# The second MLP in two sweeps over its column groups: partial sums through DRAM, weight conversions moved into the first sweep

## Chip, cores and metric

The kernel runs on one core of a Trainium2 chip. The metric is the device time of one execution in microseconds (us). The engines are TensorE (PE: matmuls; PEld: its weight loads), VectorE (DVE), ScalarE (ACT), GpSimd (POOL) and SyncE (SP), whose queue issues nearly all DMAs of this kernel.

## Reference

Three parts follow each other: an attention over the 256 channels of 6016 tokens, an MLP with squared ReLU (width 2048), and an MLP with an RMS norm and a SiLU gate (width 1536). Cut to what matters here:

```python
def _moe_ref(x, w_in, w_out):                      # first MLP
    h = np.maximum(x @ w_in, 0.0)
    return (h * h @ w_out)

def _moe2_ref(x, w_gate, w_val, w_out, rms_g):     # second MLP
    rms = np.sqrt(np.mean(x * x, axis=-1, keepdims=True) + 1e-06)
    xn = x / rms * rms_g
    g = xn @ w_gate
    silu = g * (1.0 / (1.0 + np.exp(-g)))
    val = xn @ w_val
    return (silu * val @ w_out)
```

## The kernel before, in words

The tokens are worked through in six pairs of blocks: five pairs of 2 x 512 tokens and a last one of 2 x 448 (numbered 0 to 5). The channels lie on the partitions, the tokens along the free dimension. After the attention (to about 57 us) comes the first MLP (to about 568 us), then the second (to about 1100 us).

Every fp32 value is kept as two fp32r numbers, a high and a low part, and a product of two such values takes three matmuls. In the second MLP the pair of token blocks and the halves of gate and value form a 2 x 2 problem that is done in seven products in place of eight; for it each pair has seven operands (x itself and sums of it), kept in DRAM (`xd`) with high and low part. A **visit** is the work of one pair, in 12 **groups** of 128 columns of the width. A group (`group` in `mlp2`, from L1501) has 21 matmuls of 512 columns for the seven products (L1528) and 12 "down" matmuls by the output weights (`mm3`, L110 to L112), which add to four sums in PSUM over all groups of the visit. Between them ScalarE copies banks (L1581, L1594, L1595, L1605), applies SiLU (L1601, L1638) and casts high parts (L1627), and VectorE joins products (L1606, L1615, L1620, L1641) and forms low parts (L1631). The last four down products of a visit are issued in the first group of the next; each is copied by ScalarE (L1516) into a tile `ys`, and from there transposed by VectorE (L1672) and stored (L1679).

The weights of the second MLP come as raw words and have to be converted by the kernel. Gate and value weights are cut in six chunks of 256 columns (0 to 5, one for two groups), the output weights in six parts of rows (0 to 5). A conversion is a row of steps: the load of 512 KB (L134), two decoding steps on GpSimd and ScalarE (L142, L145: step "a"), three on VectorE (L149, L153, L157: "b" and "c"), for a value chunk the sums of its halves (L303 to L308: "d" and "e"), then high parts on ScalarE (L216, L175: "h") and low parts on VectorE (L222, L182: "l"). Chunk 0 is kept in SBUF. `STREAMED = 3` and `EARLY = 3` say that chunks 1 to 3 and parts 0 to 3 are converted during the first MLP and put into DRAM (`gvd`, `w2d`), from where they are loaded at the start of the second MLP. Chunks 4 and 5 and parts 4 and 5 (late parts 0 and 1) are converted beside the groups of pair 0's visit. Their order is written out by hand: the string `SIDE2` (L1992) is a list of tokens, "4ga" being step a of the gate half of chunk 4, "0c+1load" step c of late part 0 followed by the load of late part 1, "." an empty place. `group` takes tokens from this list at five fixed places (`aside`, `asides`), each on the engine that the token names.

Of the seven operands the next visit needs, the first three (products 0, 3 and 1) are fetched behind group 4 (L2035), for odd pairs in one tile (`xs`, L1174), for even ones in single tiles (L1164); the other four follow in the last group, each as soon as the product that read its tile is done. The last pair's RMS norm and operands are made late: its first-MLP result waits in DRAM (`yd`), and in the visit of pair `XLATE = 2` the steps of `pair_norm` (L983, with L1009 and L1024) and `pair_steps` (L1086, with L1101 to L1113) are appended to the list behind group 3; in that visit the fetch of the next operands comes behind group 10. The store of its last operand stands ahead of that fetch in SP's queue:

```python
if f == (10 if p == XLATE else 4) and p + 1 < NP:
    for i in ORDER[:3]:
        fetch(p + 1, i, nxt)
```

Of the kernel before, what the change touches and what calls it, by code (L numbers as in the profile page):

```python
# [20 lines left out]
P = 128  # L21
# [7 lines left out]
def attn_moe_kernel(ctx: ExitStack, tc, q, k, v, tau, w_in, w_out, w_gate, w_val, w2, rms_g, out):  # L29
# [158 lines left out]
    HELD = 1  # L188
    EARLY = 3
    ROWS = EARLY + 1  # L190
    STREAMED = 3
    gv, gv_dram = {}, {}
# [73 lines left out]
    class LateRows(Call):  # L266
# [6 lines left out]
        def take(self):  # L273
            if "raw" not in late_tiles:
                late_tiles.update(raw=own["raw"][2].rearrange("p a n -> p (a n)").bitcast(I32), g=own["dg"][2])
            self.raw, self.g = late_tiles["raw"], late_tiles["g"]

# [1222 lines left out]

    def mlp2(p, ops, after_product, after_group, side):  # L1501
        n = blocks[2 * p][1]
        o = {}
        left, lasts = [], {}

        def down(f, t, d, ph, pl):
            def g():
                assert f // 2 < ROWS or ("w2", f // 2) in formed, f
                if f == 0:
                    o[t, d] = acc(d)[:, :n]  # L1510
                wh, wl = (tiles[w][:, f, d].rearrange("p i e -> p (i e)") for w in ("w2_h", "w2_l"))
                mm3(o[t, d], wh, wl, ph, pl, f == 0, f == NF2 - 1)
                if f == NF2 - 1 and p < NP - 1:
                    if d == 0:
                        o[t] = xp.tile([P, KC, NB], F32, tag="ys", name="ys", bufs=2)
                    nc.scalar.copy(out=o[t][:, d, :n], in_=o[t, d])  # L1516

            return g

        def group(f):  # L1520
# [75 lines left out]
            late("p2")  # L1596
            if f:
                aside("dve")
# [10 lines left out]
            if side and getattr(side[0], "takes_bank", False):  # L1609
                side.pop(0)(b0)()  # L1610
                rooted.append(f)
            elif f:
# [3 lines left out]
            if f:  # L1616
                asides()
# [66 lines left out]

        return group, left, last_down, finish

# [177 lines left out]
    def as_raw(t):  # L1864
        return t.rearrange("p a n -> p (a n)").bitcast(I32)
# [59 lines left out]
    for p in range(FIRST, NP):  # L1925
# [15 lines left out]
        def after_product(g, i):  # L1941
            if g == NF1 // 2 - 1:
                if not last and i in ORDER[3:]:
                    fetch_v(p + 1, i, nxt)
                if last and i == 0:
                    fetch(0, 4, ops0)
                if p == FIRST and i == ORDER[-1]:
                    wide_steps.pop(0)()
                    wide_steps.pop(0)()
                if p == NP - 2 and i == 0:  # L1950
                    last_chunk["vload"]()

        def after_group(g):
# [12 lines left out]
            if last:  # L1966
                if g == NF1 // 2 - 3:
                    rows["4gload"]()
                if g == NF1 // 2 - 2:
                    assert not side and not tokens, (len(side), len(tokens))  # L1970
                    for i in ORDER[:3]:
                        fetch(0, i, ops0)
                if g == NF1 // 2 - 1:
                    for i in (2, 5, 6):
                        fetch(0, i, ops0)
# [4 lines left out]
                    rows["4vload"]()  # L1980

# [6 lines left out]
    def both(*fs):  # L1988
# [12 lines left out]

    XLATE = 2
    nl = blocks[-1][1]
    y_dram = dp.tile([P, 4, NB], F32, tag="yd", name="yd")

    ops, nxt, tails = ops0, {}, []
    for p in range(NP):
        nxt = {}

        def after_product(f, i):  # L2010
            if f == NF2 - 1 and p + 1 < NP and i in ORDER[3:]:
                fetch(p + 1, i, nxt)

        def after_group(f):
            if p == 0:
                if f == 0:
                    late_calls[0].load()
                    load_w2(ROWS, ROWS)
                if f in (1, 2):
                    nc.sync.dma_start(out=f32(gv_chunk(f + 1)), in_=gv_dram[f + 1])  # L2020
                if f == 2:
                    assert summed.pop(NP - 1) == 4
                    x = xst.pop(NP - 1)
                    for i in range(4):
                        nc.sync.dma_start(out=y_dram[:, i, :nl], in_=x[:, 2 * i, :nl])
            if p == XLATE:
                if f == 0:
                    x = pair_state(NP - 1)
                    for i in range(4):
                        nc.sync.dma_start(out=x[:, 2 * i, :nl], in_=y_dram[:, i, :nl])  # L2030
                if f == 3:
                    side.extend(pair_side)
            if f == 10 and p in (0, XLATE):
                assert not side, len(side)
            if f == (10 if p == XLATE else 4) and p + 1 < NP:  # L2035
                for i in ORDER[:3]:
                    fetch(p + 1, i, nxt)

        group, left, last_down, finish = mlp2(p, ops, after_product, after_group, side)
        if tails:  # L2040
            left.append(tails[0])
        for f in range(NF2):
            group(f)
            if tails and 1 <= f < 5:
                tails[1][f - 1]()
        tails = [left.pop(), finish(0) + finish(1)]
        ops = nxt
# [47 lines left out]
```

## Time and profile before

| | us |
|---|---|
| median of 3 runs | 1111.47 (1111.43 to 1111.93) |
| span of the profiled execution, first to last instruction | 1109.2 |
| PE busy | 1099.4 |
| PEld busy | 927.8 |
| DVE busy | 801.5 |
| ACT busy | 785.5 |
| POOL busy | 64.5 |

The profiled execution's own time is the span that the page gives, 1109.2 us; the runs that give the median count 2.3 us more, which lies around it. A PE that is busy all the time is not by that working at its best, so the spacing of its matmuls and its waits have to be read beside the busy time. The granted TensorE clock is 0.999 of full speed over the span, its upper level of 2.4 GHz.

### The profile page before, as it was taken

The numbers are of one execution on the slowest core, as the hardware profiler recorded it, in microseconds if no ns is written. First come the engines' busy times: TensorE is split into PE (matmuls) and PEld (weight loads), VectorE is DVE, ScalarE is ACT, GpSimd is POOL, SyncE is SP. The second block draws the span as 40 slices with busy tenths as digits, with TensorE's granted clock in tenths as the row PEclk, the third lists the DMA queues.
The fourth block names the chain that finished last, engine by engine and source line by source line (L and its number), as shares of the span: only waits on it lengthen the run. The fifth ranks groups of instructions, "written<-read, shape, count | busy, mean of one in ns | idle before, by whom it ended". The sixth has DMA issues, their size and how long they took to land.

```text
span 1109.2 us, 14561 instructions
## 1 busy us (share of the span) xinstructions
PE 1099.4 (99%) x5148; PEld 927.8 (84%) x5148; DVE 801.5 (72%) x1242; ACT 785.5 (71%) x1430; POOL 64.5 (6%) x82
## 2 busy tenths in 40 slices
PE   9999999999999999999999999999999999999997
PEld 7978888888888888889988888888888888888996
DVE  7988857989887868979858866555875655655655
ACT  7788788888777768778777666556766556555654
POOL 2621100211000000000001000000000000000000
PEclk9999999999999999999999999999999999999999
DMA  9643223141521361471398022013042302202001
GB/s 342 219 114 96 79 74 115 57 162 67 164 65 57 142 217 52 152 254 39 126 330 301 36 76 77 20 33 97 28 164 77 95 1 76 86 3 68 20 20 33
DMA packets 105529, 117.34 MB, mean 106 GB/s; under 512 B 50672, under 2 KB 72688, under 8 KB 105072
## 3 DMA queue, kind: packets, MB, share of 16 engines
q1 hardware_dynamic: 103184, 115.57, 31.1%
q10 hardware_dynamic: 2272, 0.85, 0.3%
q8 instruction: 40, 0.66, 0.2%
q14 instruction: 33, 0.27, 0.1%
HBM read 73.27 MB, written 43.12 MB: 105 GB/s over the span
## 4 chain that ended last, share of the span: by engine, by line
PE 97%; ACT 1%; DMA 1%; DVE 1%; issue 0%; SPq 0%; DVEq 0%; ACTq 0%
PE mm L1528 30%; PE acc L110 13%; PE acc L111 13%; PE acc L112 13%; PE mm L1417 10%; PE mm L112 4%; PE mm L111 4%; PE mm L110 4%; PE mm L664 1%; PE acc L673 1%; PE acc L674 1%; PE acc L672 1%; PE mm L797 1%; DMA qraw<-in_k_dram 1%; PE acc L1658 0%
## 5 line engine op out<-in xcount | busy, mean ns | idle before, releaser
L1528 PE MATMUL mm<-p,gv 128*128 128x512 f32 (+1 forms) x1188 | 302.1, 387 | 0.0
L1528 PEld LDWEIGHTS mm<-p,gv 128*128 128x128 f32 x1188 | 221.8, 188 | 45.1 <-DVE hp L1606 1.1
L1631 DVE TENSOR_TENSOR sh<-hp,sh 128x512 fp32r<-128x512 f32 (+1 forms) x144 | 98.7, 685 | 129.2 <-ACT sh L1627 128.2
L1581 ACT COPY mm<-mm 128x512 f32<-128x512 f32 (+1 forms) x72 | 40.4, 562 | 166.5 <-PE mm L1528 161.8
L110 PE MATMUL acc<-sh,wo_h 128*128 128x512 f32 (+1 forms) x384 | 148.6, 387 | 0.0
L111 PE MATMUL acc<-sh,wo_h 128*128 128x512 f32 (+1 forms) x384 | 148.2, 386 | 0.0
L112 PE MATMUL acc<-sh,wo_l 128*128 128x512 f32 (+1 forms) x384 | 148.1, 386 | 0.0
L110 PE MATMUL acc<-sh,w_h 128*128 128x512 f32 (+1 forms) x284 | 109.5, 385 | 0.0
L111 PE MATMUL acc<-sh,w_h 128*128 128x512 f32 (+1 forms) x284 | 109.5, 385 | 0.0
L112 PE MATMUL acc<-sh,w_l 128*128 128x512 f32 (+1 forms) x284 | 109.5, 385 | 0.0
L883 DVE TENSOR_TENSOR sh<-p,sh 128x512 fp32r<-128x512 f32 x96 | 68.7, 715 | 39.9 <-ACT sh L876 36.1
L1627 ACT CAST sh<-hp 128x512 fp32r<-128x512 f32 (+1 forms) x144 | 89.1, 619 | 3.4 <-DVE hp L1615 1.9
L112 PEld LDWEIGHTS acc<-sh,wo_l 128*128 128x128 f32 x384 | 72.1, 188 | 13.8 <-DVE wo_l L182 0.3
L111 PEld LDWEIGHTS acc<-sh,wo_h 128*128 128x128 f32 x384 | 72.1, 188 | 13.5 <-DVE sh L1407 0.2
L110 PEld LDWEIGHTS acc<-sh,wo_h 128*128 128x128 f32 x384 | 72.1, 188 | 13.2
L1528 PE MATMUL mm<-xs,gv 128*128 128x512 f32 (+1 forms) x324 | 82.5, 381 | 0.0
L1615 DVE TENSOR_TENSOR hp<-mm,sg 128x512 f32<-128x512 f32 (+1 forms) x72 | 48.9, 679 | 42.2 <-PE mm L1528 41.6
L871 ACT ACTIVATE p<-mm 128x512 f32<-128x512 f32 x96 | 57.1, 595 | 28.9 <-PE mm L112 28.7
L1407 DVE TENSOR_TENSOR sh<-p,sh 128x512 fp32r<-128x512 f32 (+1 forms) x95 | 63.7, 670 | 14.2 <-ACT p L1402 5.9
L1606 DVE TENSOR_TENSOR hp<-mm,pu 128x512 f32<-128x512 f32 (+1 forms) x72 | 49.0, 681 | 29.0 <-ACT pu L1605 28.8
L1528 PEld LDWEIGHTS mm<-xs,gv 128*128 128x128 f32 x324 | 60.8, 188 | 10.2
L1398 ACT ACTIVATE sh<-p 128x512 fp32r<-128x512 f32 (+1 forms) x95 | 58.4, 614 | 9.0 <-DVE p L1467 7.4
(283 smaller groups left out, 2197.5 us busy)
## 6 DMA issues: line engine op xcount, KB each, us to landing
p<-xd SPq DMA_DIRECT2D x58, 256.0 KB, 4.1
xd<-xp SPq DMA_DIRECT2D x48, 256.0 KB, 2.3
raw<-in_moe_w_out_dram SPq DMA_DIRECT2D x11, 512.0 KB, 3.5
xd<-p SPq DMA_DIRECT2D x22, 256.0 KB, 2.2
gv<-gvd SPq DMA_DIRECT2D x3, 1792.0 KB, 11.4
out_dram<-ot SPq DMA_DIRECT2D x40, 128.0 KB, 2.3
qraw<-in_q_dram SPq DMA_DIRECT2D x13, 384.0 KB, 7.5
qraw<-in_k_dram SPq DMA_DIRECT2D x13, 384.0 KB, 7.6
```

What stands on the lines that cost most here:

```text
L110: nc.tensor.matmul(o, wh, xh, start=start, stop=False)
L111: nc.tensor.matmul(o, wh, xl, start=False, stop=False)
L112: nc.tensor.matmul(o, wl, xh, start=False, stop=stop)
L871: nc.scalar.activation(out=r, in_=o, func=AF.Relu)
L883: nc.vector.tensor_tensor(out=sl, in0=s, in1=f32(sh), op=ALU.subtract)
L1398: nc.scalar.activation(out=st["h"], in_=r, func=AF.Square)
L1407: nc.vector.tensor_tensor(out=st["l"], in0=q, in1=f32(st["h"]), op=ALU.subtract)
L1417: nc.tensor.matmul(bank, m_part(a, w, g), x, start=start and j == 0, stop=j == 2, skip_group_check=not start)
L1528: nc.tensor.matmul(bank, c[:, hl, a, fs], x, start=start and j == 0, stop=j == 2, skip_group_check=not start)
L1606: add(out=h22, in0=bh, in1=w, op=ALU.add)
L1627: nc.scalar.copy(out=parts[t][0], in_=x)
L1631: dve(out=pl, in0=x, in1=f32(ph), op=ALU.subtract)
```

## The change

The visits of the second MLP are cut in two. Pairs 0 to 3 first get a low visit with groups 0 to 3 (`low`), then pair 4 a full visit of 12 groups, then pairs 0 to 3 a high visit with groups 4 to 11, and pair 5 a full one: ten visits for six. The four sums of a low visit are copied by ScalarE as before (L1524 after), and stored to DRAM (`yp`, L1528 after). A high visit loads them back behind its sixth group (`load_sums`, L1538 after), and VectorE adds its own sums to them from PSUM (L1520 after) where ScalarE copied.

Chunks 2 to 5 and output parts 2 to 5 (late parts 0 to 3) are no longer needed before pair 4's visit, and are converted by a longer `SIDE2` during the low visits and the first groups of pair 4's. Only chunk 1 and parts 0 and 1 still go through DRAM from the first MLP. Value chunks and output parts share one raw tile `pu` (`late_raw`), so each such load stands behind the conversion that last read it. The last pair's normalisation moves to pair 4's visit, and its steps are appended behind the conversions that are still left there. The operands of pairs 0 to 3 are fetched twice. The number of matmuls stays as it is.

```diff
@@ -186,9 +186,10 @@
     HELD = 1
-    EARLY = 3
+    EARLY = 1
     ROWS = EARLY + 1
-    STREAMED = 3
+    STREAMED = 1
+    HALF = 4
@@ -271,9 +272,7 @@
         def take(self):
-            if "raw" not in late_tiles:
-                late_tiles.update(raw=own["raw"][2].rearrange("p a n -> p (a n)").bitcast(I32), g=own["dg"][2])
-            self.raw, self.g = late_tiles["raw"], late_tiles["g"]
+            self.raw, self.g = late_raw(), late_tiles["g"]
@@ -1163,11 +1162,11 @@
-    def fetch(p, i, ops):
+    def fetch(p, i, ops, odd):
...
-        if k < 3 and p % 2:
+        if k < 3 and odd:
@@ -1498,24 +1497,45 @@
-    def mlp2(p, ops, after_product, after_group, side):
+    part_dram = {}
+
+    def mlp2(p, span, ops, after_product, after_group, side):
...
+        f_first, f_last = span[0], span[-1]
+        part = f_last < NF2 - 1
...
-                if f == 0:
+                if f == f_first:
                     o[t, d] = acc(d)[:, :n]
...
-                mm3(o[t, d], wh, wl, ph, pl, f == 0, f == NF2 - 1)
-                if f == NF2 - 1 and p < NP - 1:
-                    if d == 0:
-                        o[t] = xp.tile([P, KC, NB], F32, tag="ys", name="ys", bufs=2)
-                    nc.scalar.copy(out=o[t][:, d, :n], in_=o[t, d])
+                mm3(o[t, d], wh, wl, ph, pl, f == f_first, f == f_last)
+                if f != f_last or p == NP - 1:
+                    return
+                if f_first:
+                    y = o[t][:, d, :n]
+                    nc.vector.tensor_tensor(out=y, in0=o[t, d], in1=y, op=ALU.add)
+                    return
+                if d == 0:
+                    sums_tile(t)
+                nc.scalar.copy(out=o[t][:, d, :n], in_=o[t, d])
+                if part:
+                    if p not in part_dram:
+                        part_dram[p] = dp.tile([P, 2, KC, NB], F32, tag=f"y{p}", name="yp")
+                    nc.sync.dma_start(out=part_dram[p][:, t, d, :n], in_=o[t][:, d, :n])
...
+        def load_sums():
+            for t in range(2):
+                sums_tile(t)
+                nc.sync.dma_start(out=o[t][:, :, :n], in_=part_dram[p][:, t, :, :n])
@@ -1912,8 +1932,13 @@
+    def late_raw():
+        if "raw" not in late_tiles:
+            late_tiles.update(raw=own["raw"][2].rearrange("p a n -> p (a n)").bitcast(I32), g=own["dg"][2])
+        return late_tiles["raw"]
+
     def value_home():
-        return as_raw(flat_tile(xp, "ys")), spare["g"][:, 1]
+        return late_raw(), spare["g"][:, 1]
@@ -1990,8 +2014,11 @@
     SIDE2 = (
-        "4ga 4gb . 4va 4gc+5gload 4vb . 4gh0 4vc+5vload 0a 4gl0 4vh0 4vd 4vl0 0b . 4ve 0c+1load 4vh1 5ga 4vl1 4vh2 0h 4vl2"
-        " 5gb . 0l 5va 5gc 5vb . 5gh0 5vc 1a 5gl0 5vh0 5vd 5vl0 5ve 1b . 5vh1 1c 5vl1 5vh2 1h 5vl2 1l"
+        "2ga 2gb . 2gc+3gload 2gh0 2gl0 . 2va . 2vb . 2vc 2vd 2vh0 2ve 2vl0 2vh1 . 2vl1 2vh2 2vl2+0load 3ga 3gb . 3gc+4gload"
+        " 3gh0 3gl0 . 0a 0b . 0c+3vload 0h 0l . . 3va 3vb . 3vc 3vd 3vh0 3ve 3vl0 3vh1 . 3vl1 3vh2 3vl2+1load . 4ga 4gb ."
+        " 4gc+5gload 4gh0 4gl0 . 1a 1b . 1c+4vload 1h 1l . . 4va 4vb . 4vc 4vd 4vh0 4ve 4vl0 4vh1 4vl1 4vh2 4vl2+2load ."
+        " 5ga 5gb 5gc 5gh0 5gl0 . 2a 2b . 2c+5vload 2h 2l . . 5va 5vb 5vc 5vd 5vh0 5ve 5vl0 5vh1 5vl1 5vh2"
+        " 5vl2+3load . . . 3a 3b 3c 3h 3l"
     )
@@ -1999,51 +2026,56 @@
-    XLATE = 2
...
+    low, high = range(HALF), range(HALF, NF2)
+    visits = [(p, low) for p in range(NP - 2)] + [(NP - 2, range(NF2))] + [(p, high) for p in range(NP - 2)]
+    visits.append((NP - 1, range(NF2)))
+    XLATE = NP - 2
...
-    for p in range(NP):
+    for x, (p, span) in enumerate(visits):
...
-            if p == XLATE:
+            if x == XLATE:
...
-                if f == 3:
+                if f == HALF - 1:
                     side.extend(pair_side)
...
-            if f == (10 if p == XLATE else 4) and p + 1 < NP:
+            if span[0] and f == span[0] + 5:
+                load_sums()
+            if f == (10 if x == XLATE else 2 if x == 0 else span[0] + 1) and follows is not None:
                 for i in ORDER[:3]:
-                    fetch(p + 1, i, nxt)
...
+                    fetch(follows, i, nxt, (x + 1) % 2)
...
-        for f in range(NF2):
+        for f in span:
             group(f)
...
-        tails = [left.pop(), finish(0) + finish(1)]
+        tails = [left.pop(), [] if span == low else finish(0) + finish(1)]
```

How the instructions stand, engine by engine. A row is the program line, the operation, what is written and what is read.

ScalarE where the last pair's normalisation begins, before (in pair 2's visit; `w` and `q` are its two work tiles, `xst` the pair's first-MLP result):

```order
L1601 ACTIVATE sg<-mm 128x512
L1605 COPY pu<-mm 128x512
L1009 ACTIVATE w<-xst 128x896
L1009 ACTIVATE q<-xst 128x896
L1581 COPY mm<-mm 128x512
L1627 CAST sh<-hp 128x512
```

and after, in pair 4's visit (`sg` holds the last output part that is converted, `w_h` its high part):

```order
L145 ACTIVATE pu<-pu 128x512
L175 CAST w_h<-sg 128x256 x2
L1008 ACTIVATE w<-xst 128x896
L1601 COPY mm<-mm 128x512
L1647 CAST sh<-hp 128x512
L1658 ACTIVATE sg<-sg 128x512
L1614 COPY mm<-mm 128x512
L1615 COPY pu<-mm 128x512
L1647 CAST sh<-hp 128x512
L1621 ACTIVATE sg<-mm 128x512
L1625 COPY pu<-mm 128x512
L1008 ACTIVATE q<-xst 128x896
```

The two squares stood beside each other in the same group; now the last part's conversion stands ahead of the first, and the second comes one group later.

SP's queue around the end of a visit, before, from the last load of an output part on (`xs`: the odd pair's first three operands, `p_...`: single operands, `ot`: finished output):

```order
L134 DMA pu<-in_moe_w_out_dram 128x2x512
L1174 DMA xs<-xd 128x1024 x3
L1164 DMA p_6121<-xd 128x512 x2
L1164 DMA p_6132<-xd 128x512 x2
L1164 DMA p_6146<-xd 128x512 x2
L1164 DMA p_6153<-xd 128x512 x2
L1679 DMA out_dram<-ot 32x16x64 x4
L1164 DMA p_6446<-xd 128x512 x2
L1164 DMA p_6449<-xd 128x512 x2
L1164 DMA p_6452<-xd 128x512 x2
L1679 DMA out_dram<-ot 32x16x64 x4
```

and after, at the end of a low visit (`cr`: raw gate chunk, `pu`: raw value chunk or output part, `yp`: partial sums in DRAM):

```order
L1173 DMA xs<-xd 128x1024 x3
L134 DMA cr<-in_moe_w_gate_dram 128x2x512
L1163 DMA p_6083<-xd 128x512 x2
L1163 DMA p_6094<-xd 128x512 x2
L1163 DMA p_6110<-xd 128x512 x2
L1163 DMA p_6119<-xd 128x512 x2
L134 DMA pu<-in_moe_w_val_dram 128x2x512
L1528 DMA yp<-ys 128x512 x4
L1163 DMA p_6258<-xd 128x512 x2
L1163 DMA p_6261<-xd 128x512 x2
L1163 DMA p_6264<-xd 128x512 x2
L134 DMA pu<-in_moe_w_out_dram 128x2x512
```

Raw loads and the stores of the sums now stand between the fetches of each low visit, and no output is stored there.

VectorE in the first groups of a visit whose predecessor ended with copies, before:

```order
L1606 TENSOR_TENSOR hp<-mm,pu 128x512
L1615 TENSOR_TENSOR hp<-mm,sg 128x512
L1620 TENSOR_TENSOR sg<-mm,pu 128x512
L1631 TENSOR_TENSOR sh<-hp,sh 128x512
L1641 TENSOR_TENSOR hp<-sg,hp 128x512
L1631 TENSOR_TENSOR sh<-hp,sh 128x512
L1606 TENSOR_TENSOR hp<-mm,pu 128x512
```

and after, in the first group behind a high visit (`acc_...` are the PSUM banks of the sums):

```order
L1626 TENSOR_TENSOR hp<-mm,pu 128x512
L1520 TENSOR_TENSOR ys<-acc_7761,ys 128x512
L1520 TENSOR_TENSOR ys<-acc_7765,ys 128x512
L1635 TENSOR_TENSOR hp<-mm,sg 128x512
L1640 TENSOR_TENSOR sg<-mm,pu 128x512
L1651 TENSOR_TENSOR sh<-hp,sh 128x512
L1520 TENSOR_TENSOR ys<-acc_7799,ys 128x512
L1661 TENSOR_TENSOR hp<-sg,hp 128x512
L1651 TENSOR_TENSOR sh<-hp,sh 128x512
L1520 TENSOR_TENSOR ys<-acc_7816,ys 128x512
L1626 TENSOR_TENSOR hp<-mm,pu 128x512
```

Four adds of the sums have come in, two between the steps L1626 and L1635, one ahead of L1661 and one straight ahead of the next group's L1626. (L1606, L1615, L1620, L1631 and L1641 of before are L1626, L1635, L1640, L1651 and L1661 after.)

## Rows read from the trace of the kernel before

**Rows 1.** Page, part 1: busy us of each engine, share, instructions.
```profile
PE 1099.4 (99%) x5148; PEld 927.8 (84%) x5148; DVE 801.5 (72%) x1242; ACT 785.5 (71%) x1430; POOL 64.5 (6%) x82
```
**Rows 2.** Waits of PE, whole span: us in total, times, longest us.
```profile
PE mm L664 <- DVE hl L643: 1.4, 3, 0.5
PE mm L605 <- DVE ws L601: 1.2, 1, 1.2
PE mm L112 <- DVE m_l L807: 0.8, 2, 0.5
PE mm L797 <- ACT at L762: 0.4, 1, 0.4
```
**Rows 3.** Chain of waits, its longest pieces: start us, us, what.
```profile
664.68 2.72 PE mm L1528 x12
672.16 2.81 PE mm L1528 x12
679.73 2.72 PE mm L1528 x12
...
762.01 2.79 PE mm L1528 x12
...
792.14 3.10 PE mm L1528 x12
```
**Rows 4.** Stretches of 20 us: PE, PEld, DVE, ACT, POOL busy (x); clock, DMA share, GB/s.
```profile
300.00:320.00 20.00, 20.00 (x90) 16.53 (x90) 15.43 (x25) 16.16 (x29) 0.00 (x0) 1.00 0.50 156
580.00:600.00 20.00, 20.00 (x89) 16.48 (x89) 16.45 (x29) 13.75 (x27) 1.72 (x2) 1.00 0.96 362
...
620.00:640.00 20.00, 20.00 (x90) 16.57 (x89) 17.08 (x30) 13.40 (x26) 0.00 (x0) 1.00 0.01 2
720.00:740.00 20.00, 20.00 (x90) 16.57 (x89) 10.78 (x16) 12.01 (x23) 0.00 (x0) 1.00 0.00 0
```
**Rows 5.** Timeline of ACT at a visit's end: start us, us, instruction.
```profile
670.28 0.61 ACT L1601 ACTIVATE sg<-mm 128x512 f32<-128x512 f32 x1
670.77 0.60 ACT L1516 COPY ys<-acc 128x512 f32<-128x512 f32 x1
671.24 0.62 ACT L1605 COPY pu<-mm 128x512 f32<-128x512 f32 x1
```
**Rows 6.** Timeline of DVE, there and a group later; behind [ the idle time before.
```profile
671.89 0.69 DVE L1606 TENSOR_TENSOR hp<-mm,pu 128x512 f32<-128x512 f32 x1 [0.77 <-ACT pu L1605]
...
679.03 0.69 DVE L1606 TENSOR_TENSOR hp<-mm,pu 128x512 f32<-128x512 f32 x1 [0.34 <-ACT pu L1605]
```
**Rows 7.** Page, part 5: ACT's first copy of a group.
```profile
L1581 ACT COPY mm<-mm 128x512 f32<-128x512 f32 (+1 forms) x72 | 40.4, 562 | 166.5 <-PE mm L1528 161.8
```
**Rows 8.** DMA, 600 to 640 us: GB/s by us, then issues.
```profile
GB/s 396 389 43 7 0 0 47 217 420 426 426 410 152 0 0 0 0 0 0 0 0 0 0 0 0 0 0 0 16 0 8 0 0 0 0 0 0 8 0 0
...
xs<-xd SPq DMA_DIRECT2D x3, 512.0 KB, 5.1
pu<-in_moe_w_out_dram SPq DMA_DIRECT2D x1, 512.0 KB, 3.5
```
**Rows 9.** Timeline of SP's queue, 815 to 850 us.
```profile
825.57 0.32 SPq L1113 DMA_DIRECT2D xd<-xp  x1
825.94 1.41 SPq L1174 DMA_DIRECT2D xs<-xd  x3
834.74 5.14 SPq L1164 DMA_DIRECT2D p<-xd  x8
```
**Rows 10.** Tile xs, 815 to 850 us: its three fetches.
```profile
DMA to landing us min/median/max: 4.1/4.8/6.8
```
**Rows 11.** Timeline of PE, start of the visit after that.
```profile
838.62 1.52 PE L1528 MATMUL mm<-xs,gv 128*128 128x512 f32 x6
...
840.66 0.84 PE L1528 MATMUL mm<-xs,gv 128*128 128x512 f32 x3
841.35 0.84 PE L1528 MATMUL mm<-p,gv 128*128 128x512 f32 x3
```

More of the change, by code (lines that the diff above doesn't have):

```diff
@@ L1596, in group @@
             late("p2")
-            if f:
+            if not first:
                 aside("dve")
@@ L1611, in group @@
                 rooted.append(f)
-            elif f:
+            elif not first:
                 asides()
@@ L1615, in group @@
             dve(out=h21, in0=bv, in1=sg1, op=ALU.mult)
-            if f:
+            if not first:
                 asides()
@@ L1683, in finish @@
             return [turned(0), lambda: (turned(1)(), store())]
-        return group, left, last_down, finish
+        return group, left, last_down, finish, load_sums
     def run(up, down, n, lag, hooks, mid={}, beside={}):
@@ L1945, in after_product @@
                 if last and i == 0:
-                    fetch(0, 4, ops0)
+                    fetch(0, 4, ops0, False)
                 if p == FIRST and i == ORDER[-1]:
@@ L1967, in after_group @@
                 if g == NF1 // 2 - 3:
-                    rows["4gload"]()
+                    rows[f"{STREAMED + 1}gload"]()
                 if g == NF1 // 2 - 2:
@@ L1971, in after_group @@
                     for i in ORDER[:3]:
-                        fetch(0, i, ops0)
+                        fetch(0, i, ops0, False)
                 if g == NF1 // 2 - 1:
                     for i in (2, 5, 6):
-                        fetch(0, i, ops0)
+                        fetch(0, i, ops0, False)
                     for x in "hl":
@@ L1979, in after_group @@
                     nc.sync.dma_start(out=f32(gv_chunk(1)), in_=gv_dram[1])
-                    rows["4vload"]()
         mlp1_pair(p, ops1, side, after_product, after_group)
@@ L2008, in attn_moe_kernel @@
         nxt = {}
+        follows = visits[x + 1][0] if x + 1 < len(visits) else None
         def after_product(f, i):
-            if f == NF2 - 1 and p + 1 < NP and i in ORDER[3:]:
-                fetch(p + 1, i, nxt)
+            if f == span[-1] and follows is not None and i in ORDER[3:]:
+                fetch(follows, i, nxt, (x + 1) % 2)
         def after_group(f):
-            if p == 0:
+            if x == 0:
                 if f == 0:
[L2017 to L2021, printed above, removed]
+                    load_w2(ROWS, 2)
+                    rows[f"{STREAMED + 1}vload"]()
+                if f == 1:
@@ L2022, in after_group @@
                     assert summed.pop(NP - 1) == 4
-                    x = xst.pop(NP - 1)
+                    y = xst.pop(NP - 1)
                     for i in range(4):
-                        nc.sync.dma_start(out=y_dram[:, i, :nl], in_=x[:, 2 * i, :nl])
-            if p == XLATE:
+                        nc.sync.dma_start(out=y_dram[:, i, :nl], in_=y[:, 2 * i, :nl])
+            if x == XLATE:
                 if f == 0:
-                    x = pair_state(NP - 1)
+                    y = pair_state(NP - 1)
@@ L2029, in after_group @@
                     for i in range(4):
-                        nc.sync.dma_start(out=x[:, 2 * i, :nl], in_=y_dram[:, i, :nl])
-                if f == 3:
+                        nc.sync.dma_start(out=y[:, 2 * i, :nl], in_=y_dram[:, i, :nl])
+                if f == HALF - 1:
                     side.extend(pair_side)
-            if f == 10 and p in (0, XLATE):
-                assert not side, len(side)
-            if f == (10 if p == XLATE else 4) and p + 1 < NP:
+                if f == 10:
+                    assert not side, len(side)
@@ L2036, in after_group @@
+            if span[0] and f == span[0] + 5:
+                load_sums()
+            if f == (10 if x == XLATE else 2 if x == 0 else span[0] + 1) and follows is not None:
                 for i in ORDER[:3]:
-                    fetch(p + 1, i, nxt)
-        group, left, last_down, finish = mlp2(p, ops, after_product, after_group, side)
+                    fetch(follows, i, nxt, (x + 1) % 2)
+        group, left, last_down, finish, load_sums = mlp2(p, span, ops, after_product, after_group, side)
@@ L2040, in attn_moe_kernel @@
         if tails:
             left.append(tails[0])
-        for f in range(NF2):
+        for f in span:
             group(f)
-            if tails and 1 <= f < 5:
-                tails[1][f - 1]()
-        tails = [left.pop(), finish(0) + finish(1)]
+            if tails and 1 <= f - span[0] < 5 and tails[1]:
+                tails[1].pop(0)()
+        tails = [left.pop(), [] if span == low else finish(0) + finish(1)]
         ops = nxt
```

2 lines of the change are left out of this document (added).

## Prediction, on record before the changed kernel ran

> **What bounds the kernel now.** I read the page first, then TensorE's waits, then the chain of waits, and last the stretches around each place that the change touches. The page has TensorE (PE) busy for 1099.4 of 1109.2 us [rows 1]. The view of its waits names four lines, together 3.8 us, all of them in the front part of the program [rows 2]: in both MLPs no wait of TensorE is long enough to be listed. What is left there is seen in the chain. A group's twelve matmuls take 2.72 us, which is 0.227 us each, and a group of 33 starts 7.48 us after the one before (664.68 to 672.16) [rows 3]. At the ends of visits the same piece takes 2.79 to 2.81 us, so each costs 0.07 to 0.09 us, and beside the normalisation of the last pair it takes 3.10 us, 0.38 us more [rows 3]. So the second MLP of before gives at most 5 x 0.09 + 0.38 = 0.8 us back. The first MLP shows no more: at 300 us the matmuls follow each other as densely as at 620 or 720 us, 90 in 20 us, although VectorE (DVE) and ScalarE (ACT) convert weights there [rows 4]. Taking conversions out of the first MLP can therefore hardly gain, and the question is what the second MLP now loses. About 0.2% (2.2 us) can be told from no change; it is the bound of the chances below.
>
> The page's own execution spans 1109.2 us. The median of the runs shown is 1111.47 us, 2.27 us more, which I take as lying around the span and unchanged. All terms are added to the median.
>
> **TensorE's own work.** The matmuls stay the same in number and form; a sum that starts anew in the second sweep starts in PSUM and is joined to its first part on VectorE. Term: 0.
>
> **Conversions in the first sweep.** Two chunks and two row parts were converted in some ten groups at 575 to 650 us; now four and four in about twenty. The density stays. There VectorE was busy 16.45 to 17.08 us and ScalarE 13.4 to 13.8 us of 20, against 10.78 and 12.01 us where nothing is converted, and the matmul count was the same [rows 4]. So I take 0. The bound above: VectorE comes within 15% of full, and ScalarE now also works for copies to DRAM; if each of the four visits loses as much as the normalisation did, 4 x 0.38 = 1.5 us. Below, nothing: there is no stall to remove but those of the visit's first group.
>
> **Value chunks and row parts through one raw tile.** They now share one tile, so a load can be issued only when the previous user is converted, and by the order of the rows some 16 to 22 matmuls stand between that and the conversion that asks for it, 3.6 to 5.0 us by 0.227 us. A load of the same size took 3.5 us alone [rows 8]; beside other transfers three fetches of that size took 4.1 to 6.8 us [rows 10]. Three value loads stand so (for chunks 3, 4 and 5). What is queued behind a late one is ScalarE's next copy, for which TensorE waits; ScalarE sat idle 161.8 us ahead of its 72 such copies, 2.2 us each, for no other reason than TensorE [rows 7], and this takes up most of it. I take 0.1 us for each, 0.3 us; the bounds are 0 and, with each 1 us late beyond its cover, 3 us. The fetch of 3.5 us is the nearer row, since the first sweep has few other transfers in flight at those points.
>
> **Stores of the partial sums, and their loads.** A low visit stores four blocks of 256 KB and a high visit fetches two of 512 KB, at its sixth group, three groups (over 20 us) ahead of the adds. They lie beside TensorE's work as the operand fetches do. A low visit takes 4 x 7.5 = 30 us and moves operands (3.67 MB), sums (1.05 MB) and raw weights (1.6 MB), some 6.3 MB: 210 GB/s. While the same kinds of transfers were in flight, the rows have 410 to 426 GB/s [rows 8]. Term 0, at most 0.5 us. The Trainium skill (page "DMA: Bandwidth & Descriptors", section "Bandwidth") speaks against so much traffic: it gives about 358 GB/s as what memory grants one core, and says that this side binds. The rows of this trace have more, 426 GB/s; by either figure the low visit's average fits.
>
> **Ends of visits.** There were five and there are nine. Five end in copies by ScalarE as before (four low ones and pair 4): 5 x 0.08 = 0.4 us, as before. There the copy of one sum (670.77) delays the next copy (671.24) and that VectorE's step (671.89) [rows 5, 6], so that the last product starts late. At the four new ends of the second sweep VectorE adds instead. ScalarE is then free, but an add of about 0.69 us, as long as its neighbours [rows 6], stands straight ahead of that same step on VectorE. In a plain group the step starts 0.34 us after VectorE fell idle [rows 6], so 0.69 us of work leaves some 0.35 us, part of which falls before the operand is there. I take 0.1 us each, 0.4 us; bounds 0 and 4 x 0.35 = 1.4 us.
>
> **Normalisation of the last pair.** It moves from the third visit to pair 4's and starts behind the last converted row part, one group later than it could before. Its cost of 0.38 us moves with it. But its last store now ends one group (7.48 us) nearer to the visit's end, and the fetch of the next visit's first three operands comes behind that store on SP's queue. Before, the last store was issued at 825.57, the three fetches from 825.94 on [rows 9], and they landed after 4.1, 4.8 and 6.8 us [rows 10]. The products that read them came at 838.62, about 839.3 and 840.66 [rows 11]. Shifted by 7.48 us against the same products, the fetches are issued at 833.4, 833.9 and 834.3 and land, in the order of those times, at 837.5, 838.7 and 841.1: the third is 0.4 us late. The fetches for the other four operands, from 834.74 on [rows 9], then run beside these three instead of after them. Until the fourth is read at 841.35 [rows 11] the two lots make 2.1 MB, which at 420 GB/s [rows 8] take 5.0 us from about 834.9: 839.9, in time. I take 0.5 us; bounds 0 (all land as in the best case) and 3.5 us (below). By the 358 GB/s of that page of the Trainium skill the 2.1 MB would take 5.9 us, until 840.8, still in time, and the sum would not change.
>
> **First MLP and its end.** Fewer chunks go through DRAM and fewer loads stand at the start of the second MLP. No listed wait was caused by these loads [rows 2], and 300 us shows no loss [rows 4]: I take -0.1 us. At most it is -1 us, about what the ends and the normalisation of the second MLP cost before, since nothing of that size is seen in the first.
>
> Sum: 0.3 + 0.4 + 0.5 - 0.1 = +1.1 us, **1112.6 us**: no change that can be told.
>
> **Rivals.**
> (1) *The fetch behind pair 4's last store becomes the bound (slower).* Seven operands, 3.67 MB with stores beside them some 4.1 MB, must pass in about 12.9 us from 833.4 until the last product of the next visit's first group has its operand: 318 GB/s. From there on it decides. For it: operand fetches in the rows do not run at 420 GB/s all the time, since each pair is issued only as its product is done (eight issues spread over 5.14 us [rows 9]). At 275 GB/s they take 14.9 us, 2.0 us late; at 250 GB/s 16.4 us, 3.5 us late. Against it: the rows' 410 to 426 GB/s with four fetches queued [rows 8]. With the other terms 1111.5 + 0.6 + 2.0 to 3.5: 1114.1 to 1115.6, say 1114.9 us.
> (2) *Late raw loads hold ScalarE, or VectorE's queue holds both, in the first sweep.* With each of three value loads 1 us beyond its cover, +3 us in place of 0.3: 1114.2 us. For it: one raw tile in place of separate ones. Against it: ScalarE's 2.2 us before each copy [rows 7], and the same density of work without loss at 580 to 640 us [rows 4].
> (3) *The relief counts (faster).* If the first MLP hides 1 us, and the new ends cost nothing: 1110.5 us. To pass 0.2% it would need 2.2 us, which no wait of TensorE in either MLP offers [rows 2, 3].
> (4) *The sweep moves no time at all,* all covers hold: 1111.4 us.
>
> **How the numbers follow.** My forecast 0.55, and (4) 0.17: both within 0.2%. Rival (1) 0.12, (2) 0.10, (3) 0.06, of which half by 0.2%. Of the slower rivals nearly all is over 1113.7 us. That gives 0.03 faster, 0.75 same, 0.22 slower. For 8 in 10 the range goes from 1110.9 (part of (3)) to 1115.0 us (most of (1) and (2)); the bounds of the single terms lie inside as far as they don't fall together.
>
> **What the profile after would show.** Right: TensorE still 90 matmuls in 20 us in the first MLP and in the first sweep; the pieces of the chain at 2.72 us but at visit ends, nine of them, each under 0.2 us; one piece lengthened by about 0.4 us beside the normalisation and one or two by some 0.5 us at the end of pair 4's visit, with the third fetched operand landing at the moment its product starts; in the view of TensorE's waits still only the lines of the front part, or at most one on a fetched operand. Wrong: if ScalarE's conversion step idles on loads of value chunks for more than about 2 us and a product waits behind it (2); if TensorE waits over 2 us on operands at the end of pair 4's visit (1); or if stalls of some tenths recur in every group of the first sweep, which would say that VectorE or ScalarE is full.

## The result: slower by 0.7%

The changed kernel takes 1119.22 us (median of 4 runs, 1118.62 to 1120.54), the kernel before 1111.45 us (4 runs, 1111.15 to 1111.93). The ratio is 1.0070, with a 95% interval from 1.0056 to 1.0084. The forecast was 1112.6 us, with a range up to 1115.0: the time lies 4.2 us above it. The profiled execution spans 1116.8 us where the one of before spans 1109.2.

First the page's line of busy time, to be read against [rows 1]:

```profile
PE 1101.9 (99%) x5148; PEld 928.0 (83%) x5148; DVE 809.3 (72%) x1266; ACT 786.8 (70%) x1430; POOL 39.4 (4%) x74
```

TensorE is busy for 99% again. 2.5 us of the added 7.6 us even count as busy. The page's first line says nothing of what happened. The view of TensorE's waits (us in total, times, longest us) does, beside [rows 2]:

```profile
PE mm L1548 <- ACT mm L1601: 5.8, 6, 1.6
PE mm L604 <- DVE ws L600: 1.2, 1, 1.2
PE mm L112 <- DVE m_l L806: 0.8, 2, 0.5
PE mm L663 <- DVE hl L642: 0.4, 1, 0.4
PE mm L796 <- ACT at L761: 0.4, 1, 0.4
```

A line has come in that was not there: products (L1548) wait for ScalarE's first bank copy of a group (L1601), six times, 5.8 us. Where they lie follows from counting through the matmul records of both traces. At the 2700th matmul, near the end of the first MLP, the changed kernel is 0.98 us ahead (0.83 us of it by the 60th matmul of the attention; TensorE waits 1.4 us for VectorE's `hl` there in [rows 2] and 0.4 us here). At the 3600th, after pair 4's normalisation, it is 7.78 us behind, and at the last 7.49 us. So the loss of 8.8 us lies between 577 and 750 us, in the first sweep and the first half of pair 4's visit, and the second sweep gains 0.3 us, which is what the normalisation of the last pair had cost there, at 792 us of the kernel before. By the spacing of matmul starts above 0.227 us the six stalls are 1.3, 1.1, 1.2, 0.6, 1.9 and 1.3 us, at 584, 623, 655, 694, 702 and 734 us, together 7.4 us; five small ones (0.1 to 0.4 us), at the ends of the four low visits and at 747 us, make most of the rest.

The first stall in TensorE's timeline (start us, us, instruction, in brackets the idle time before it and what ended it):

```profile
581.71 2.44 PE L1548 MATMUL mm<-p,gv 128*128 128x512 f32 x10
...
584.44 0.39 PE L112 MATMUL acc<-sh,w_l 128*128 128x512 f32 x1
585.86 1.42 PE L1548 MATMUL mm<-p,gv 128*128 128x512 f32 x5 [1.03 <-ACT mm L1601]
```

ScalarE at the same place:

```profile
580.40 0.60 ACT L1625 COPY pu<-mm 128x512 f32<-128x512 f32 x1
580.86 0.70 ACT L145 ACTIVATE cr<-cr 128x512 int32<-128x512 uint32 x1
584.70 0.62 ACT L217 CAST gv<-cr 128x512 fp32r<-128x512 f32 x1 [3.13 <-DVE cr L157]
585.23 0.58 ACT L1601 COPY mm<-mm 128x512 f32<-128x512 f32 x1
```

and VectorE:

```profile
581.64 0.42 DVE L149 TENSOR_SCALAR cr<-cr 128x512 int32<-128x512 int32 x1
582.18 0.69 DVE L153 CUSTOM_DVE_ANT_0 cr<-cr 128x1024 uint16<-128x1024 uint16 x1
582.79 0.68 DVE L1635 TENSOR_TENSOR hp<-mm,sg 128x512 f32<-128x512 f32 x1
583.39 0.68 DVE L1640 TENSOR_TENSOR sg<-mm,pu 128x512 f32<-128x512 f32 x1
583.99 0.68 DVE L157 SCALAR_TENSOR_TENSOR cr<-cr 128x512 int32<-128x512 int32 x1
```

ScalarE does its decoding step of gate chunk 2 (L145, "a"), and its next instruction is the cast of the same chunk's high part (L217, "h"). The cast needs what VectorE's last decoding step (L157, "c") writes, and VectorE comes to that only behind two other decoding steps and two products of the group (L1635, L1640): 3.13 us. The copy L1601 stands behind the cast. Its operand was there (the product's matmuls ended about 584.2), but it starts at 585.23, and TensorE waits 1.03 us for it. The other five stalls show a cast of the same kind, at gate chunks 4 and 5 and late parts 0, 2 and 3, but at two of them more stands in the stretch. At 702 us two copies of sums come ahead of step a. At 734 us the first square of the normalisation (L1008) follows the cast:

```profile
733.43 0.71 ACT L175 CAST w_h<-sg 128x256 fp32r<-128x256 f32 x2 [2.53 <-DVE sg L157]
734.05 0.94 ACT L1008 ACTIVATE w<-xst 128x896 f32<-128x896 f32 x1
734.90 0.57 ACT L1601 COPY mm<-mm 128x512 f32<-128x512 f32 x1
```

The groups of ScalarE's casts of gate chunks and output parts (busy us, mean ns, then idle time before them and what ended it), in the changed kernel from 575 to 752 us:

```profile
L145 ACT ACTIVATE pu<-pu 128x512 int32<-128x512 uint32 x8 | 5.5, 681 | 0.4 <-DMA pu<-in_moe_w_val_dram 0.4
...
L217 ACT CAST gv<-cr 128x512 fp32r<-128x512 f32 (+1 forms) x8 | 4.1, 513 | 15.4 <-DVE cr L157 15.4
L175 ACT CAST w_h<-sg 128x256 fp32r<-128x256 f32 x8 | 2.9, 404 | 8.2 <-DVE sg L157 8.2
```

and in the kernel before, from 575 to 665 us:

```profile
L216 ACT CAST gv<-cr 128x512 fp32r<-128x512 f32 (+1 forms) x8 | 4.6, 570 | 2.5 <-DVE cr L157 2.5
...
L175 ACT CAST w_h<-sg 128x256 fp32r<-128x256 f32 x4 | 1.4, 407 | 0.0
```

23.6 us of ScalarE's time went into waiting for VectorE's decoding, where it was 2.5 us. Not all of the 23.6 us cost something. The six casts above waited 17.5 us of it; three others, at 598, 615 and 678 us, waited 1.35, 2.38 and 2.38 us, and TensorE lost nothing behind them. The one at 615 us is gate chunk 3's:

```profile
611.84 0.62 ACT L1625 COPY pu<-mm 128x512 f32<-128x512 f32 x1
614.83 0.62 ACT L217 CAST gv<-cr 128x512 fp32r<-128x512 f32 x1 [2.38 <-DVE cr L157]
615.35 0.58 ACT L1601 COPY mm<-mm 128x512 f32<-128x512 f32 x1
```

Its step a had run a group earlier (606.76), and the copy starts 2.9 us after the end of L1625. At 585 us that is 4.2 us.

The wait on a raw load, which my second rival named, is 0.4 us in all. In the string `SIDE2` the cause can be read: before, "4gc+5gload 4vb . 4gh0" puts two tokens between step c and the cast; after, it is "2gc+3gload 2gh0". The string alone does not decide it: chunk 3 has the same tokens in the same order, but they fall into other groups. Since all ScalarE tokens of a group fall between L1625 and the next group's L1601, a chunk whose steps a and h are both taken in one group waits for its whole decoding inside that stretch.

What ran as forecast or better: the fetch behind pair 4's normalisation. SP's queue there, then the three landings, beside [rows 9, 10]:

```profile
780.83 0.32 SPq L1112 DMA_DIRECT2D xd<-xp  x1
781.20 1.42 SPq L1173 DMA_DIRECT2D xs<-xd  x3
```

```profile
DMA to landing us min/median/max: 4.0/4.7/5.4
```

The first product that reads them starts at 786.4, 5.2 us after the first issue, as worked out in the prediction, and none waits. An end of the second sweep, on VectorE and then on TensorE:

```profile
856.44 0.68 DVE L1520 TENSOR_TENSOR ys<-acc,ys 128x512 f32<-128x512 f32 x1
...
859.02 0.68 DVE L1520 TENSOR_TENSOR ys<-acc,ys 128x512 f32<-128x512 f32 x1
859.62 0.68 DVE L1626 TENSOR_TENSOR hp<-mm,pu 128x512 f32<-128x512 f32 x1
```

```profile
859.93 2.88 PE L1548 MATMUL mm<-p,gv 128*128 128x512 f32 x12
862.65 0.39 PE L110 MATMUL acc<-sh,w_h 128*128 128x512 f32 x1
```

The last add stands right ahead of L1626, as the order said, but L1626 starts at 859.62 with its operand ready, and the twelve matmuls follow each other at 0.227 us (859.93 to 862.65). These ends cost nothing that the spacing shows, less than the 0.07 to 0.09 us of ScalarE's copies in [rows 3].

### The profile page after: what moved, and what is told of

It reads as the page before. It is cut to its first block, busy times and chain, and to the rows that moved or that the text cites. A ratio compares the mean times of both kernels' runs of the same rounds, so it can differ in the third digit from the quotient of the medians.

```text
span 1116.8 us, 14686 instructions
## 1 busy us (share of the span) xinstructions
PE 1101.9 (99%) x5148; PEld 928.0 (83%) x5148; DVE 809.3 (72%) x1266; ACT 786.8 (70%) x1430; POOL 39.4 (4%) x74
## 5 line engine op out<-in xcount | busy, mean ns | idle before, releaser
L1548 PE MATMUL mm<-p,gv 128*128 128x512 f32 (+1 forms) x1188 | 303.1, 388 | 5.2 <-ACT mm L1601 5.0
L1548 PEld LDWEIGHTS mm<-p,gv 128*128 128x128 f32 x1188 | 221.5, 188 | 52.7 <-ACT mm L1601 7.5
L1651 DVE TENSOR_TENSOR sh<-hp,sh 128x512 fp32r<-128x512 f32 (+1 forms) x144 | 98.5, 684 | 116.9 <-ACT sh L1647 116.0
L1601 ACT COPY mm<-mm 128x512 f32<-128x512 f32 (+1 forms) x72 | 40.5, 563 | 146.5 <-PE mm L1548 137.1
L1548 PE MATMUL mm<-xs,gv 128*128 128x512 f32 (+1 forms) x324 | 82.8, 382 | 0.8 <-ACT mm L1601 0.8
L112 PEld LDWEIGHTS acc<-sh,wo_l 128*128 128x128 f32 x384 | 72.1, 188 | 13.8 <-DVE wo_l L182 0.2
L1635 DVE TENSOR_TENSOR hp<-mm,sg 128x512 f32<-128x512 f32 (+1 forms) x72 | 48.8, 677 | 34.0 <-PE mm L1548 33.5
L1548 PEld LDWEIGHTS mm<-xs,gv 128*128 128x128 f32 x324 | 60.7, 188 | 11.5 <-ACT mm L1601 1.4
L1626 DVE TENSOR_TENSOR hp<-mm,pu 128x512 f32<-128x512 f32 (+1 forms) x72 | 48.9, 679 | 28.0 <-ACT pu L1625 28.0
```

Of the source, the lines that this page charges most:

```text
L1548: nc.tensor.matmul(bank, c[:, hl, a, fs], x, start=start and j == 0, stop=j == 2, skip_group_check=not start)
L1626: add(out=h22, in0=bh, in1=w, op=ALU.add)
L1651: dve(out=pl, in0=x, in1=f32(ph), op=ALU.subtract)
```

## Experiments

Theory A is the one above: order on ScalarE. Rival B: VectorE is too full in the first sweep, whatever the order. Rival C: the added transfers. All runs are compared with the kernel before on the same chip.

**casts_later.** In `SIDE2` alone, tokens are moved so that none of the six casts waits through a whole decoding (cut to the places that differ):

```diff
- 2gc+3gload 2gh0 2gl0 . 2va .
+ 2gc+3gload . 2gh0 2gl0 2va .
- 0c+3vload 0h 0l . . 3va
+ 0c+3vload . 0h 0l . 3va
- 4gc+5gload 4gh0 4gl0 . 1a 1b .
+ 4gc+5gload . 4gh0 4gl0 1a 1b .
- 5gc 5gh0 5gl0 . 2a 2b . 2c+5vload 2h 2l . . 5va
+ 5gc . . 5gh0 5gl0 2a 2b 2c+5vload . 2h 2l 5va
```

(By the last line, late part 3's steps a and b also come in the group ahead of its steps c and h.)

> The changed kernel with only the list of side steps edited: every high-part cast that stood in the same group as its own decoding (gate chunks 2, 4 and 5, late parts 0, 2 and 3) comes one group later, or its decoding one group earlier. Same work, same transfers. Theory A (ScalarE waits in that cast for VectorE's decoding, and its next bank copy, for which TensorE waits, is queued behind): the stalls of 0.6 to 1.9 us at 584, 623, 655, 694, 702 and 734 us of the changed kernel's trace go, some 7 us, and the time is 1111.5 to 1113.0 us, the span about 1110. Rival B (VectorE is simply too full in the first sweep): the stalls move elsewhere, 1117 to 1119 us. Rival C (the added transfers delay loads or operands): nothing changes, 1118.5 to 1120 us.

Measured: 1112.86 us (11 runs, 1111.93 to 1113.52) against 1111.65, ratio 1.0009 (1.0001 to 1.0018). Some 6.4 us are back. Two casts that were not moved still wait 2.38 us each, at 614 and 674 us, and cost nothing again. TensorE's waits from 570 to 760 us:

```profile
PE mm L1548 <- ACT mm L1614: 0.4, 1, 0.4
PE mm L1548 <- ACT mm L1601: 0.2, 1, 0.2
PE mm L1548 <- ACT pu L1625: 0.2, 1, 0.2
```

Rival B is decided by the busy time of the stretch from 580 us to the same work's end (PE, PEld, DVE, ACT, POOL busy), in the changed kernel:

```profile
580.00:746.00 166.00, 160.01 (x695) 128.83 (x694) 124.17 (x205) 116.64 (x223) 8.59 (x12) 1.00 0.48 161
```

and in casts_later:

```profile
580.00:740.00 160.00, 159.22 (x696) 129.34 (x695) 124.92 (x206) 117.82 (x225) 8.04 (x12) 1.00 0.48 167
```

VectorE does the same 124 to 125 us of work, once in 166 us with the stalls and once in 160 us nearly without them. It was not too full. C falls with it, as the same transfers are made.

**gate_casts_later.** Only the three gate casts are moved, as in the first, third and fourth lines of that diff, with "2c+5vload 2h 2l . . 5va" left as it was.

> The changed kernel, only the casts of gate chunks 2, 4 and 5 moved one group later; the casts of late parts 0, 2 and 3 stay directly behind their decoding. Theory A: three of the six stalls go (1.3, 1.2 and 0.6 us), the others stay: about 1116.1 us (1115.5 to 1116.8). B and C: 1118 to 1120 us.

Measured: 1117.80 us (5 runs), ratio 1.0056 (1.0043 to 1.0069). By the medians it is 1.4 us faster than the changed kernel instead of the 3.1 us that three stalls had cost, 1.0 us above the expected range, and the two intervals overlap. The stalls at 584, 655 and 694 us are gone from the trace, and those of late parts 0 and 3 stay, as expected. But moving 5gh0 put it into the group at the end of pair 3's low visit. There ScalarE shows:

```profile
694.97 1.27 ACT L1524 COPY ys<-acc 128x512 f32<-128x512 f32 x2
696.13 0.62 ACT L217 CAST gv<-cr 128x512 fp32r<-128x512 f32 x1
696.65 0.68 ACT L145 ACTIVATE pu<-pu 128x512 int32<-128x512 uint32 x1
700.46 0.71 ACT L175 CAST w_h<-sg 128x256 fp32r<-128x256 f32 x2 [3.13 <-DVE sg L157]
701.08 0.58 ACT L1601 COPY mm<-mm 128x512 f32<-128x512 f32 x1
```

Two copies of sums, the moved cast, late part 2's step a and its cast with its wait now stand in one stretch ahead of one L1601, which starts 4.4 us after the step a began. The loss there grew from 2.3 to 4.6 us, and it has two parts. The stall itself is 3.0 us where it was 1.9. The other 1.6 us are no wait: TensorE stood idle for 2.70 us, and from 702.5 to 705.9 us its granted clock is 0.50, its level of 1.2 GHz, so that eight matmuls follow each other at 0.43 us in place of 0.227. On TensorE, and then the stretch as a whole (busy time as above, the granted clock third from the end):

```profile
701.71 2.28 PE L1548 MATMUL mm<-p,gv 128*128 128x512 f32 x6 [2.70 <-ACT mm L1601]
```

```profile
702.50:705.90 3.40, 3.40 (x9) 2.64 (x8) 2.85 (x5) 3.30 (x7) 0.66 (x1) 0.50 0.53 205
```

The expected mechanism held at the three gate casts; its sum left out that the token lands somewhere, and that a longer stall can cost clock behind it. Whether the clock falls there in every run is not shown.

**casts_behind_copy.** Five casts (all but late part 3) are issued just behind the next group's L1601 instead of just ahead:

```diff
             cp(out=bu, in_=b0)
+            while behind:
+                behind.pop(0)()
...
+    for y in ("2gh0", "0h", "4gh0", "5gh0", "2h"):
+        rows[y] = only("act", lambda f=rows[y]: behind.append(f))
```

(and "5gh0 5gl0 ." becomes "5gh0 . 5gl0").

> The changed kernel with the order of VectorE, SP and the list as it was, but five casts (gate chunks 2, 4, 5 and late parts 0 and 2) issued on ScalarE just behind the next group's first bank copy in place of just ahead of it. The casts then run hardly later than before. Theory A: five stalls of 6.1 us in all go, a little is lost where the cast delays ScalarE's next cast of products: 1113.0 to 1114.5 us. B: VectorE has the same work at the same places, 1118 to 1120 us. C: 1118.5 to 1120 us.

Measured: 1115.29 us (6 runs), ratio 1.0036 (1.0024 to 1.0048): 3.9 us back, and 0.8 us above the expected range. ScalarE at gate chunk 2:

```profile
584.79 0.57 ACT L1601 COPY mm<-mm 128x512 f32<-128x512 f32 x1 [1.98 <-PE mm L1548]
585.93 0.62 ACT L217 CAST gv<-cr 128x512 fp32r<-128x512 f32 x1 [0.57 <-DVE cr L157]
586.46 0.61 ACT L1649 CAST sh<-hp 128x512 fp32r<-128x512 f32 x1
```

The copy no longer waits for VectorE, and the cast still does, for 0.57 us, which costs TensorE nothing at that point and 0.3 us some matmuls later. Four stalls of 4.2 us shrank to 0.4 us in all. The fifth, late part 2 at the end of pair 3's visit, only falls from 2.3 to 1.75 us. Its copy (698.93) was held by VectorE's L1635 step (L1637 there), since step a, behind two copies of sums, came late to VectorE. TensorE's wait there is for the next copy (L1616), which stands behind that late copy and behind the cast with its 0.57 us of waiting:

```profile
702.84 0.98 PE L1548 MATMUL mm<-p,gv 128*128 128x512 f32 x3 [0.94 <-ACT mm L1616]
```

How much of this piece is the cast's was not separated. 0.7 us more were lost at 576 us, where a product waited 0.5 us for an operand fetch; no other trace shows that. So at the four places inside a visit the cast's own lateness costs 0.3 us at most; what counts there is the copy queued behind it. The Trainium skill (page "PSUM — Partial Sum Buffer", section "Engine vs sequencer instructions") says that the queues of ScalarE, VectorE and GpSimd are strictly first in, first out; the traces agree, as the copy with its operand ready starts 0.53 us after the cast in one order (584.70, 585.23) and 1.14 us ahead of it in the other (584.79, 585.93).

**no_partial_sums.** The sums of the low visits are neither stored nor loaded, and ScalarE copies at the ends of the high visits; the low groups' part of the output of pairs 0 to 3 is left out.

```diff
-                if f_first:
-                    y = o[t][:, d, :n]
-                    nc.vector.tensor_tensor(out=y, in0=o[t, d], in1=y, op=ALU.add)
-                    return
...
-                if part:
-                    if p not in part_dram:
-                        part_dram[p] = dp.tile([P, 2, KC, NB], F32, tag=f"y{p}", name="yp")
-                    nc.sync.dma_start(out=part_dram[p][:, t, d, :n], in_=o[t][:, d, :n])
...
-            if span[0] and f == span[0] + 5:
-                load_sums()
```

> The changed kernel without the stores of the low visits' sums, without their loads, and with ScalarE's copy in place of VectorE's add at the ends of the high visits: the low groups' part of the output of pairs 0 to 3 is left out. Theory A: same stalls, 1118.8 to 1119.6 us. Rival C, as far as these 8.4 MB are the cause: 1115 us or less.

Measured: 1121.03 us (4 runs), ratio 1.0083 (1.0069 to 1.0097), so not faster; C falls for these 8.4 MB. The stalls are the same:

```profile
PE mm L1540 <- ACT mm L1593: 5.9, 6, 1.6
```

That it is slower by 1.8 us than the changed kernel was not expected. The two intervals overlap; in the traces 0.8 us lie in the attention and 1.3 us in the last pair's visit, which the edit does not touch. Those 1.3 us are no stall: from the second group of that visit on, the matmuls (448 columns) follow each other at 0.207 us in place of 0.203, at a granted clock of 1.00. The trace of before_casts_close (next) shows the same, the other six do not. Why stays open.

**before_casts_close.** The kernel before, with the same fault put in at three places (the other steps of chunk 5 and late part 1 are regrouped for it):

```diff
- 4gc+5gload 4vb . 4gh0 4vc+5vload
+ 4gc+5gload 4gh0 4vb . 4vc+5vload
- 4vh1 5ga 4vl1 4vh2 0h 4vl2 5gb . 0l 5va 5gc 5vb . 5gh0 5vc
+ 4vh1 . 4vl1 4vh2 0h 4vl2 . . 0l 5ga 5gb . 5gc 5gh0 5gl0 5va 5vb 5vc
- 1a 5gl0 5vh0 5vd 5vl0 5ve 1b . 5vh1 1c 5vl1 5vh2 1h 5vl2 1l
+ 5vh0 5vd 5vl0 5ve . 5vh1 5vl1 5vh2 5vl2 1a 1b . 1c 1h 1l
```

> The kernel of before (one sweep, its own transfers), only its list of side steps edited: the casts of gate chunks 4 and 5 and of late part 1 put directly behind their decoding, into the same group. Theory A: three stalls of 1 to 1.9 us come into a kernel that has none: 1114.5 to 1116.5 us. Rivals B and C: two chunks and two parts leave VectorE and the queue room, 1111 to 1112 us.

Measured: 1114.29 us (11 runs, 1113.34 to 1116.80) against 1111.73, ratio 1.0024 (1.0015 to 1.0033). The loss is 2.6 us, and the time lies 0.2 us below the expected range, nearer to it than to the 1111 to 1112 us of B and C. ScalarE's and TensorE's waits from 570 to 660 us:

```profile
ACT gv L216 <- DVE cr L157: 10.3, 4, 3.1
...
ACT w_h L175 <- DVE sg L157: 3.1, 1, 3.1
```

```profile
PE mm L1528 <- ACT mm L1581: 2.9, 3, 1.4
```

Three waits of TensorE on the same copy have come into a kernel that had none [rows 2], without two sweeps and without one added byte. By the spacing of the starts they are 1.7, 1.0 and 1.1 us, at 586, 625 and 649 us. That is more than the median lost; the traced execution took 1116.80 us, 2.5 us more than the median, 1.3 us of it in the last visit, and what the stalls are in the others is not shown. In kind, A is shown in both directions: with the casts moved away four of the six stalls go and the other two shrink (casts_later), and with casts moved close to their decoding three come.

**casts_off_the_end.** From casts_later, gate chunk 5's decoding starts a group earlier, so that nothing of it falls into the end of pair 3's visit, and one empty place follows the last late part:

```diff
- 4vl2+2load . 5ga 5gb 5gc . . 5gh0 5gl0 2a 2b 2c+5vload
+ 4vl2+2load 5ga 5gb . 5gc 5gh0 5gl0 . 2a 2b . 2c+5vload
- 3c 3h 3l
+ 3c 3h 3l .
```

> As casts_later, and besides: the decoding of gate chunk 5 starts a group earlier, so that its cast leaves the window at the end of pair 3's low visit, where ScalarE also copies two sums and VectorE's low part waited for the cast (stall of 1.2 us at 698 us there); an empty place behind the last late part keeps the second square of the normalisation out of the group of the first (0.4 us at 729 us). Theory A (what is left is order too): 1.2 to 1.6 us less than casts_later, 1111.0 to 1112.0 us, equal to the kernel before within 0.1%. Rival B (the rest is VectorE's load): no gain, 1112.5 to 1113.5 us. Under neither does it beat the kernel before by more than 0.5 us, since TensorE waited nowhere there for what the change takes away.

Measured: 1111.70 us (11 runs, 1110.88 to 1112.44) against 1110.66 on its chip, ratio 1.0010 (1.0000 to 1.0019): no gain over casts_later by the ratios. Its time lies in the range expected by A only because the kernel before is 1 us faster on that chip, too. In the trace the stall at 698 us fell from 1.2 to 0.1 us and the one at 729 us went, but 0.4 us came in at 703 us, and the second MLP as a whole lost 0.75 us less than in casts_later, which is less than the intervals can tell. TensorE has no listed wait there any more; what is left are pieces of 0.1 to 0.4 us at the visit ends of the first sweep. Whether they are order too, or VectorE's load (rival B for this rest), is not decided, and whether they can be ordered away was not tried. No version here beats the kernel before.

## Why the prediction was wrong

**The step that failed** is "Conversions in the first sweep": "The density stays. ... So I take 0", with 1.5 us as its upper bound. It measured 7.4 us in six stalls. In its place the runs showed ScalarE's bank copy held behind a cast that waits for VectorE's whole decoding. The rows that the step rested on [rows 4] were read rightly, but for one that they leave out (600 to 620 us, with ScalarE busy for 15.08 us, above the 13.4 to 13.8 us given), and VectorE was indeed not too full. But a busy share does not say in which order two engines meet. What counted was how many ScalarE and VectorE steps lie between a cast and its decoding within one stretch of ScalarE's queue. The evidence was at hand ahead of the run: the order of ScalarE after the change shows L145, L175 and L1008 in a row, and I read it only for the place of L1008. The size of its price could be had, too. VectorE's chain behind step a is five instructions of 0.42 to 0.69 us, 3.1 us, and ScalarE has 2.2 us to spare ahead of a group's first copy [rows 7], out of which step a and the cast, 0.6 us each, must be paid. That makes an estimate of 3.1 + 1.2 - 2.2 = 2.1 us for each such cast, where 0.6 to 1.9 us were measured. The prediction's own sign of trouble in this sweep was stalls in every group, for an engine that is full; six single ones it did not foresee.

**Value chunks and row parts through one raw tile** (0.3 us): ScalarE waited 0.4 us on a value load, once. Raw loads landed in 3.7 to 3.8 us by the median. The cover held.

**Rival (2)** had the right engine and the right queue behind it, but the wrong thing waited for: not a late load but VectorE's own decoding. Its heading does name VectorE's queue, but no price was worked out for that half. Its 1114.2 us also leave out terms of the sum: 1112.6 - 0.3 + 3 is 1115.3 us, just above the stated range. Rival (3) has the same slip; with the other terms it comes to 1111.3 us.

**Stores and loads of the sums** (0): right. **First MLP** (-0.1 us): the two traces stay within 0.2 us of each other from the 60th to the 2700th matmul; nothing was gained there. **Ends of visits** (+0.4 us for the four new ends): they cost nothing. The ends of the four low visits cost 0.10, 0.14, 0.33 and 0.39 us where 0.08 us each was taken, and pair 4's end nothing. **Normalisation and the fetch behind it** (0.5 us, up to 3.5): the issue times came out within 0.1 us, the landings were 4.0 to 5.4 us, and no product waited; rival (1) did not occur. The 1.3 us at 734 us lie at the normalisation's first step: the cast of late part 3 waited 2.5 us there, and the first square, 0.94 us, followed ahead of the copy. In casts_later the cast waits 1.36 us there, both squares follow (0.95 and 0.94 us), and 0.4 us are lost; so the wait for the whole decoding was most of it. The steps after that cost 0.2 us, at 747 us, where before they had cost 0.35 us at 792 us.

With the order mended, casts_later has +1.2 us (1112.86 against 1111.65, with an interval from 0.1 to 2.0 us) beside the +1.1 us of the sum. That is luck and no support for its terms: the pieces in the trace are 0.3 us at the end of pair 2's low visit, 1.2 us at the end of pair 3's and 0.4 us at the squares, while the raw loads, the ends of the high visits and the fetch behind the normalisation, which made up the sum, cost nothing there.

## What to carry to other kernels

Where side work of two engines is dealt out by a list, look at what stands directly behind an instruction that waits for the other engine, and count the instructions of that engine in between; busy shares don't show it. A cast in the same group as its own whole decoding cost 0.6 to 1.9 us each time here; inside a visit one group's distance cost nothing, with the same work. After moving such a token, look at where it lands: the end of a visit with its copies had no room for it. And look at the granted clock behind a long stall: one of them cost 1.6 us more than the wait.

## What the runs showed of the chip that was not expected

The added 14.7 MB of operand fetches and 8.4 MB of sums did no harm: in the first sweep the loads of 512 KB landed in 3.7 to 5.3 us by the median, not later than the 3.5 and 5.1 us of [rows 8] by more than 0.3 us, and leaving the sums out gave nothing back. Behind an idle time of 2.70 us TensorE's granted clock was 0.50 for 3.4 us (gate_casts_later). The 448-column matmuls of the last visit were spaced 0.207 us in two traces and 0.203 us in six. Executions of the same instructions differ by up to 0.96 us from the kernel before already at the 60th matmul, in the attention's start; it is a shift that stays to the end and has to be taken out when two traces are compared.
